# A convolution by FFT, a SiLU layer and a soft mixture of experts in one kernel: the exchange of the hidden layer's halves starts one chunk later, and one of its copies moves in every batch

## The chip, the cores and the metric

The kernel runs on one core of a Trainium2 chip. The metric is the device time of one execution in microseconds, the median of several runs.

## What is computed

The reference does three things in a row, all in 32-bit floats, on an input x of 8 batches, 3072 tokens and 256 channels:

```python
X = np.fft.rfft(x, axis=1)                    # convolution along the tokens, by a filter of frequencies
y = np.fft.irfft(X * (filt_r + 1j*filt_i)[None], n=3072, axis=1)
h = y.reshape(24576, 256) @ w_in              # hidden layer of 2048
z = (h / (1 + np.exp(-h))) @ w_out            # SiLU, back to 256
logits = z @ phi                              # 32 slots: 8 experts of 4
d = softmax(logits, axis=0)                   # over all 24576 tokens
s = (d.T @ z).reshape(8, 4, 256)              # what each slot sees
o = relu(s @ w1) @ w2                         # each expert on its 4 slots
out = softmax(logits, axis=1) @ o             # over the slots, for each token
```

## The kernel before

**Chunks.** The tokens are taken in 48 chunks of 512, six to a batch. For a chunk `c`, `mat4` (tile `py`) ends the inverse transform, and then come 16 blocks m = 0 to 15 of the hidden layer: `hidden` (six matmuls into `ph`, weights and activations split in a rounded part and a rest), `act` (ScalarE, SiLU, tile `g`) and `turn` (VectorE, transposes 32x32 blocks of `g` into the tile `X` of the chunk). `logits` (tile `pl`) sums `g` into 32 logits a token; they are exponentiated against a running maximum (tile `e`), go to DRAM (`ed`, function `spread0`) and come back spread over the partitions as `E` (`spread1`). `dsum` (tile `pd`) multiplies `E` with `X`, so that the sum over all tokens is taken of the hidden layer, and `update` adds it to `acc`. `dsum` of a chunk runs late in the next chunk, at its step 10.9.

**The exchange.** Where `swapped(c)` holds, the halves of `X` are exchanged between neighbouring groups of 32 partitions before `dsum`, so that it takes 32 products of 64x32 tiles of TensorE, eight at a time; elsewhere it takes 64 products of 32x32 tiles, 16 at a time. (A product of 32-bit floats counts as two instructions.) The exchange is made in two halves of eight blocks, and each half takes two copies of four blocks on GpSimd into the buffer `swap` (`swap_copy`, line 695), then two transfers `X<-X` (`swap_up`, line 699) and two transfers `X<-swap` (`swap_down`, line 704), issued by SyncE. There is one such buffer (tag S, 8 KB a partition): the third copy of a chunk waits until the `X<-swap` of its first half has been read. Before chunk 2 the same buffer holds `E_01`, the E of the chunks without exchange; the E of the others has a tag of its own and half the bytes.

**The convolution.** While the six chunks of a batch go through, the transform of the next batch is computed beside them (`fft_plan`). Its stage 2 runs in four groups Q = 0 to 3 of four tiles U: `mat2` (TensorE, tile `px`, from `a`, which comes from DRAM), `act2` (ScalarE, tile `sw`), `direct2` (VectorE, `y` from `px` and the filter `f`), `cross2` (GpSimd, `sw` times `f`, line 221) and `add2` (VectorE, `y` plus `sw`, line 360). Stage 3, `mat3` (tile `pb`), multiplies the four `y`. For Q = 0 stage 2 stands late in a batch's second chunk (c % 6 == 1) and its stage 3 early in the third.

**The order of the work.** It is written out by hand: `at(t, fn, ...)` notes a call with a time in steps, one step being one hidden block and 16 a chunk; the calls are sorted by t and issued in that order, and each engine works through its own instructions in order, as does the DMA queue of SyncE. So t is not a time but a place in each queue. In the second chunk of a batch, whose first step is `t0`, the copies stand at t0 + 7.7, 8.47, 12.5 and 16.47, the transfers up at t0 + 9.25 and 17.95, down at t0 + 11.2 and 19.35; the four cross products of Q = 0 stand at t0 + 12.5 (placed just ahead of the copy with the same time), 13.1, 14.0 and 14.2, their sums at 14.3, the stage 3 at 17.9.

The names of tiles in the profile are those given above; line 66 is the helper of all matmuls.

Of the kernel before, what the change touches and what calls it, by code (L numbers as in the profile page):

```python
# [9 lines left out]
F32 = mybir.dt.float32  # L10
# [7 lines left out]
P = 128  # L18
# [4 lines left out]
S = 32  # L23
# [4 lines left out]
CPB = NJ // JC  # L28
# [8 lines left out]
BUFS = dict(X=2, yT=2, g=11, L=2, nm=4, S=1, E2=2, lall=2, ct=1, cm=1,  # L37
            ld=3, c=2, ch=2, xh=2, a=1, f=2, y=2, ev8=1, bl=1, bp=1, dl=1, wt=3)
# [8 lines left out]
def fftconv_moe_softmoe(ctx, tc, x, cmat, chl, dmat, dmat0, emat, gmat, filt, sign, w_in, w_outT, w_out,  # L47
# [4 lines left out]
    NCHUNK = NB * CPB  # L52

    cst = ctx.enter_context(tc.tile_pool(name="cst", bufs=1))
    wk = ctx.enter_context(tc.tile_pool(name="wk", bufs=2))
# [9 lines left out]
    def mm(o, l, r, start, stop):  # L65
        T.matmul(o, lhsT=l, rhs=r, start=start, stop=stop)  # L66
# [75 lines left out]
    def at(t, fn, *args):  # L142
        plan.append((t, len(plan), fn, args))
# [542 lines left out]
    swap = {}  # L686

    def swapped(c):
        return 2 <= c < NCHUNK - 1

    def swap_copy(c, m):
        if m % 8 == 0:
# [65 lines left out]
    def spread1(c):  # L758
        if c == NCHUNK - 1:
            tail["S"] = wk.tile([P, 2048], F32, tag="S", bufs=BUFS["S"], name="tail_S")  # L760
            soft[c] = E = tail["S"][:, 0:512].rearrange("p (q f) -> p q f", q=4)
            t = et.pop(c)
            for q in range(4):
                pe = ps_h.tile([P, P], F32, tag="ph", name=f"pe_{q}")
                mm(pe, fold[S * q:S * q + S, :], t[S * q:S * q + S, 1], True, True)
                if q % 2:
                    V.tensor_copy(E[:, q, :], pe)
                else:
                    A.activation(E[:, q, :], pe, AF.Copy)
        elif not swapped(c):  # L770
            if c == 0:
                tail["E"] = wk.tile([P, 2, 4, P], F32, tag="S", bufs=BUFS["S"], name="E_01")
            soft[c] = E = tail["E"][:, c]
            ed = edt.pop(c)
            for a in range(4):
                DQ.dma_start(E[S * a:S * a + S], ed.rearrange("q i f -> i q f"))
        else:
            soft[c] = E = wk.tile([P, 2, P], F32, tag="E2", bufs=BUFS["E2"], name=f"E_{c}")
            ed = edt.pop(c)
            for a in range(4):  # L780
                h = 2 * (a % 2)
                DQ.dma_start(E[S * a:S * a + S], ed[h:h + 2].rearrange("q i f -> i q f"))
# [3 lines left out]
    def dsum(c):  # L786
        pdt[c] = {a: pool.tile([P, NM, 32], F32, tag=tag, name=f"pd_{c}_{a}")
                  for a, (pool, tag) in zip((0, 2, 1, 3), FOUR[:3] + ((ps_h, "ph"),))}
        X, E = xt.pop(c), soft[c]
        if not swapped(c):  # L790
            for B in range(4):
                for a in range(4):
                    s = slice(S * a, S * a + S)
                    for q in range(4):
                        mm(pdt[c][a][S * q:S * q + S], E[s, q, S * B:S * B + S], X[s, q // 2, :, 4 * (q % 2) + B, :],
                           B == 0, B == 3)
            return
        for x in range(2):
            for k in range(2):
                for R in range(2):  # L800
                    s = slice(64 * R, 64 * R + 64)
                    for g in range(4):
                        q, B = g % 2, g // 2 + 2 * k
                        mm(pdt[c][2 * R + x][S * g:S * g + S], E[s, q, S * B:S * B + S], X[s, x, :, 4 * q + B, :],
                           k == 0, k == 1)
# [67 lines left out]
    tail = {"w1": [], "w2": [], "t": []}  # L873
# [61 lines left out]
    for c in range(NCHUNK):  # L935
        t0 = 16 * c
        if c > 0:
            at(t0 - 16 + 6.9 if c < 3 or c % CPB == 0 else t0 - 19, loadd, c)
            at(t0 - 16 + 5.6 if c < 3 or c % CPB == 0 else t0 - 18.9, load3, c)
            at(t0 - 16 + 9.6 if c > 1 else 11.6, fly, c)  # L940
        ty = t0 - 16 + (VIS3 + 0.003 + (1.5 if c == 2 else 0) if c > 1 else 11.94) if c else -2
        for h in range(2):
            at(ty + 0.001 * h, mat4, c, h)
            at(ty + (0.002 * h + 0.01 if c else 0.2 * h + 0.55), out4, c, h)
        for m in range(NM):
            t = t0 + m
            late = c == 0 and m > 11
            at((11.8 + 0.01 * (m - 12) if m < 15 else 11.965) if late else t, hidden, c, m)
            at(11.97 + 0.001 * (m - 12) if c == 0 and m > 10 else t + (0.8995 if m in (1, 10) else 1.45 if (c, m) == (1, 11) else 1), act, c, m)
            te = max(t + 1.45 if m not in (1, 10) else t + 0.8996, (16.6 + 0.8 * (m - 5) if m > 4 else 11.7, 20.6 + 0.1 * m)[c] if c < 2 else 0)  # L950
            at(te, turn, c, m)
        copies, ups, downs = (((43.5, 43.6, 48.4, 48.47), (44.5, 49.95), (46.6, 51.35)) if c == 2 else
                              ((t0 + 7.7, t0 + 8.47, t0 + 12.5, t0 + 16.47), (t0 + 9.25, t0 + 17.95),
                               (t0 + 11.2, t0 + 19.35)))
        for i in range(4 if swapped(c) else 0):
            at(copies[i], swap_copy, c, 4 * i)
            if i < 2:
                at(ups[i], swap_up, c, 8 * i)
                at(downs[i], swap_down, c, 8 * i)
        at(t0 + VIS3 + 0.002 + (1.5 if c == 1 else 0) if c else 11.96, logits, c, 0)  # L960
        t1 = t0 + 16 + (VIS1 if c else 4.6)
        at(t1 + 0.002, logits, c, 1)
        if c == NCHUNK - 1:
            at(t1 + 0.0025, keep, 9)
        at(t1 + 0.003, soft0, c)
        if c < NCHUNK - 1:
            at(t1 + 0.00305, exp_early)
        at(t1 + 0.0031, soft1, c)
        at(t1 + 0.06, soft2, c)
        at(t1 + 1.1, soft3, c)  # L970
        if c < NCHUNK - 1:
            at(t1 + 1.5, spread0, c)
        at(t1 + (1.6 if swapped(c) else 3.3 if c < NCHUNK - 1 else 1.5), spread1, c)
        t3 = t0 + 16 + VIS3 + (1.5 if c == 0 else 0)
        at(t3, dsum, c)
        if c < NCHUNK - 1:
            at(t3 + 0.001, update, c)
        if c % 4 == 3:
            last = c == NCHUNK - 1
            if last:  # L980
                at(t0 + 16.95, exp_table)
            else:
                at(t1 + (11.2 if (c + 1) % CPB else 19.1), cprep, c // 4)
                at(t1 + {1: 43.8, 3: 27.8, 5: 19.1}[(c + 2) % CPB], cfin, c // 4)
                if c // 4 < NK - 2:
                    at(t1 + {1: 43.8, 3: 27.8, 5: 19.1}[(c + 2) % CPB] + 5, cstore, c // 4)
    E = mybir.EngineType
# [289 lines left out]
def _build(arrays):  # L1277
    import concourse.bacc as bacc

    nc = bacc.Bacc("TRN2", target_bir_lowering=False, num_devices=1, dynamic_dma_scratch_size=1024)  # L1280
    args = {}
    for name, a in arrays.items():
        args[name] = nc.dram_tensor(f"in_{name}_dram", a.shape, mybir.dt.from_np(a.dtype), kind="ExternalInput").ap()
    o = nc.dram_tensor("out_0_dram", arrays["x"].shape, F32, kind="ExternalOutput").ap()
    with tile.TileContext(nc, schedule_with_timeline_sim=True) as tc:  # L1285
        fftconv_moe_softmoe(tc, out=o, **args)
    return nc
# [10 lines left out]
```

## Time and profile before

| | us |
|---|---|
| median of 3 runs (1876.95 to 1885.63) | 1878.9 |
| the profiled execution | 1874.56 |
| its span, first to last instruction | 1872.4 |
| TensorE busy in it | 1799.6 (96%) |
| VectorE / ScalarE / GpSimd busy | 1278.1 / 953.7 / 450.2 |
| mean granted clock of TensorE | 0.979 |

In the profile PE is TensorE, DVE VectorE, ACT ScalarE, POOL GpSimd, SP SyncE, and SPq the instructions by which SyncE's queue issues transfers. A line gives the place in the kernel, the engine, the operation and the tiles as "written<-read". "Idle before" is the time in which the engine stood still ahead of an instruction, and behind the arrow stands what ended it. The granted clock is a share of full speed.

### The profile page before, as it was taken

How to read it: one execution, taken by the hardware profiler on the slowest of the kernel's cores; microseconds unless marked ns; L12 is line 12 of the kernel's file. 1: busy time of each engine (PE TensorE's matmuls, PEld its weight loads, DVE VectorE, ACT ScalarE, POOL GpSimd, SP SyncE). 2: the span in 40 equal slices, each digit the busy share in tenths (PEclk: the TensorE clock that was granted, in tenths of full speed). 3: DMA queues.
4: the chain of work that ended last, by engine and by line, in shares of the span. 5: the costliest groups of instructions: out<-in, count | busy, mean ns of one | idle time of the engine just before them, and what ended most of it. 6: DMA issues, size and time to landing. Idle time of an engine off the chain costs nothing. (4 is left out here: it accounts for less than half of the span.)

```text
span 1872.4 us, 45508 instructions
## 1 busy us (share of the span) xinstructions
PE 1799.6 (96%) x18538; PEld 1347.2 (72%) x18538; DVE 1278.1 (68%) x2279; ACT 953.7 (51%) x1831; POOL 450.2 (24%) x380
## 2 busy tenths in 40 slices
PE   7899999999999999989999999999999999999995
PEld 6677577767776778767786777767786777777754
DVE  3597677678667766677676876677667776776543
ACT  2554556456455556456455556456554645454433
POOL 0201323133132323232232323232332321111000
PEclk9899999999999999999999999999999999999996
DMA  9965657676677658776486647676586655445689
GB/s 323 316 214 172 190 152 234 196 213 179 174 214 206 184 142 229 213 210 188 138 246 198 200 123 226 211 204 204 140 240 180 201 157 157 120 142 144 228 313 397
DMA packets 210932, 379.91 MB, mean 203 GB/s; under 512 B 24508, under 2 KB 130724, under 8 KB 196004
## 3 DMA queue, kind: packets, MB, share of 16 engines
q1 hardware_dynamic: 177244, 330.46, 58.5%
q10 hardware_dynamic: 33480, 46.56, 7.5%
q8 instruction: 146, 2.39, 0.5%
q14 instruction: 62, 0.51, 0.1%
HBM read 192.82 MB, written 91.83 MB: 152 GB/s over the span
## 5 line engine op out<-in xcount | busy, mean ns | idle before, releaser
L66 PE MATMUL ph<-yT,w_hl 128*128 128x512 f32 x4608 | 1092.4, 393 | 0.6 <-DVE yT L653 0.2
L66 PEld LDWEIGHTS ph<-yT,w_hl 128*128 128x128 f32 x4608 | 852.4, 188 | 200.9 <-issue 27.3
L684 DVE STREAM_TRANSPOSE X<-g 128x512 f32<-128x512 f32 x768 | 517.0, 696 | 233.7 <-ACT g L674 229.7
L674 ACT ACTIVATE g<-ph 128x512 f32<-128x512 f32 x768 | 450.1, 602 | 337.5 <-PE ph L66 256.0
L695 POOL COPY swap<-X 128x1024 f32<-128x1024 f32 x180 | 198.0, 1101 | 773.7 <-DVE X L684 514.7
L221 POOL TENSOR_TENSOR sw<-sw,f 128x512 f32<-128x512 f32 x123 | 162.1, 1332 | 401.6 <-ACT sw L215 385.1
L66 PEld LDWEIGHTS pl<-g,wp 128*32 128x32 f32 x6144 | 164.2, 111 | 71.8 <-issue 66.3
L652 ACT ACTIVATE yT<-py 128x512 fp32r<-128x512 f32 x96 | 57.3, 597 | 308.7 <-PE py L66 308.7
L66 PE MATMUL pl<-g,wp 128*32 128x128 f32 x6144 | 190.6, 276 | 0.6 <-DVE wp L138 0.6
L66 PE MATMUL pd<-X,E 64*32 64x512 f32 (+1 forms) x3136 | 178.5, 597 | 4.6 <-DMA E<-ed 4.4
L812 DVE SCALAR_TENSOR_TENSOR acc<-acc,nm,pd 128x512 f32<-128x512 f32 x184 | 124.9, 734 | 9.2 <-PE pd L66 9.1
L66 PEld LDWEIGHTS pd<-X,E 64*32 64x32 f32 (+1 forms) x3136 | 57.8, 107 | 99.4 <-issue 89.8
L360 DVE TENSOR_TENSOR y<-y,sw 128x512 f32<-128x512 f32 x112 | 106.7, 992 | 21.1 <-POOL sw L221 21.1
L279 POOL TENSOR_TENSOR xh<-x,xh 128x512 fp32r<-128x512 f32 x72 | 92.9, 1290 | 116.0 <-DVE xh L278 97.5
L653 DVE TENSOR_TENSOR yT<-py,yT 128x512 fp32r<-128x512 f32 x96 | 66.3, 691 | 71.9 <-ACT yT L652 71.9
L218 DVE TENSOR_TENSOR y<-px,f 128x512 f32<-128x512 f32 x124 | 82.0, 679 | 33.9 <-PE px L66 28.4
L370 ACT ACTIVATE eb<-pb 128x512 f32<-128x512 f32 x112 | 57.8, 603 | 41.2 <-PE pb L66 41.2
L214 ACT ACTIVATE sw<-px,sg 128x256 f32<-128x256 f32 x123 | 60.0, 488 | 32.7 <-PE px L66 14.5
L66 PE MATMUL py<-d,b 128*128 128x128 f32 x416 | 65.8, 282 | 5.5 <-DMA b<-hop 4.7
L66 PEld LDWEIGHTS pa<-xh,ch 128*128 128x128 f32 x432 | 61.1, 189 | 10.7 <-POOL xh L279 4.4
L66 PE MATMUL pa<-xh,ch 128*128 128x256 f32 x432 | 64.8, 283 | 2.6 <-POOL xh L279 2.4
L66 PE MATMUL pb<-y,gm 32*32 32x512 f32 (+1 forms) x1008 | 50.9, 654 | 14.1 <-DVE y L360 14.1
(157 smaller groups left out, 1346.5 us busy)
## 6 DMA issues: line engine op xcount, KB each, us to landing
X<-X SPq DMA_DIRECT2D x180, 256.0 KB, 3.7
X<-swap SPq DMA_DIRECT2D x180, 256.0 KB, 4.2
f<-in_filt_dram SPq DMA_DIRECT2D x128, 256.0 KB, 4.1
a<-s SPq DMA_DIRECT2D x64, 512.0 KB, 5.4
s<-eb SPq DMA_DIRECT2D x60, 512.0 KB, 5.1
out_dram<-ots SPq DMA_DIRECT2D x23, 1024.0 KB, 11.9
b<-s SPq DMA_DIRECT2D x160, 128.0 KB, 4.9
x<-in_x_dram ACTq DMA_DIRECT2D x72, 256.0 KB, 5.0
```

The lines of the kernel that those rows point to most:

```text
L66: T.matmul(o, lhsT=l, rhs=r, start=start, stop=stop)
L214: A.activation(sw[:, 0, :], p[:, 1, :], AF.Copy, scale=sg[:, s:s + 1])
L218: V.tensor_tensor(y, p, f[:, 0, :].unsqueeze(1).to_broadcast([P, 2, CH]), op=ALU.mult)
L221: G.tensor_tensor(sw, sw, f[:, 1, :].unsqueeze(1).to_broadcast([P, 2, CH]), op=ALU.mult)
L279: G.tensor_tensor(h[:, 1, :], tf, h[:, 0, :], op=ALU.subtract)
L360: V.tensor_tensor(y, y, st.pop(("sw", Q, U)), op=ALU.add)
L370: A.activation(st["eb"][:, q], p, AF.Copy)
L653: V.tensor_tensor(y[:, half, 1, :], py, y[:, half, 0, :], op=ALU.subtract)
L674: A.activation(g, pht.pop((c, m)), AF.Silu)
L684: V.transpose(xt[c][:, :, m].rearrange("p h b j -> p h (b j)"), gt[c, m].rearrange("p (h f) -> p h f", h=2))
L695: G.tensor_copy(t[:, m % 8:m % 8 + 4], xt[c][:, 0, m:m + 4].rearrange("p m b j -> p m (b j)"))
L812: V.scalar_tensor_tensor(out=acc[:, :, a, :], in0=acc[:, :, a, :], scalar=mrun[c][:, 3:4], in1=p, op0=ALU.mult, op1=ALU.add)
```

## The change

Three edits in the written order, no new function. The exchange starts with chunk 3 instead of 2. Chunk 2's E goes into the tile of the chunks 0 and 1, which gets a third part, and its `dsum` takes 16 tiles; by the rule for such chunks its `spread1` stands 1.7 steps later. Chunk 3's exchange, now the first, gets the special times that chunk 2's had: its first two copies stand behind chunk 2's `dsum` (step 58.9). And in every second chunk of a batch from chunk 7 on the third copy moves from t0 + 12.5 to t0 + 16.465, next to the fourth.

```diff
     def swapped(c):
-        return 2 <= c < NCHUNK - 1
+        return 3 <= c < NCHUNK - 1
...
         elif not swapped(c):
             if c == 0:
-                tail["E"] = wk.tile([P, 2, 4, P], F32, tag="S", bufs=BUFS["S"], name="E_01")
+                tail["E"] = wk.tile([P, 3, 4, P], F32, tag="S", bufs=BUFS["S"], name="E_012")
             soft[c] = E = tail["E"][:, c]
...
-        copies, ups, downs = (((43.5, 43.6, 48.4, 48.47), (44.5, 49.95), (46.6, 51.35)) if c == 2 else
-                              ((t0 + 7.7, t0 + 8.47, t0 + 12.5, t0 + 16.47), (t0 + 9.25, t0 + 17.95),
-                               (t0 + 11.2, t0 + 19.35)))
+        copies, ups, downs = (((59.5, 59.6, 63.5, 64.47), (60.4, 65.95), (62.2, 67.35)) if c == 3 else
+                              ((t0 + 7.7, t0 + 8.47, t0 + (16.465 if c % CPB == 1 else 12.5), t0 + 16.47),
+                               (t0 + 9.25, t0 + 17.95), (t0 + 11.2, t0 + 19.35)))
```

## Rows read from the trace of the kernel before

**Rows 1.** TensorE's waits: engine, tile, releaser, us in total, times, longest
```profile
PE pb L66 <- DVE y L360: 14.1, 12, 2.2
```
**Rows 2.** Timeline, PE, 371 to 403: start, us, instructions, idle before
```profile
371.09 8.48 PE L66 MATMUL ph<-yT,w_hl 128*128 128x512 f32 x36
380.72 1.09 PE L66 MATMUL pb<-y,gm 32*32 32x256 f32 x16 [1.15 <-DVE y L360]
382.99 1.94 PE L66 MATMUL pb<-y,gm 32*32 32x512 f32 x18 [1.18 <-DVE y L360]
...
387.52 1.17 PE L66 MATMUL px<-a,em 24*32 24x512 f32 x32
...
401.08 2.38 PE L66 MATMUL pd<-X,E 64*32 64x512 f32 x40
```
**Rows 3.** Timeline, DVE, same stretch
```profile
375.32 0.65 DVE L360 TENSOR_TENSOR y<-y,sw 128x512 f32<-128x512 f32 x1
378.91 4.02 DVE L360 TENSOR_TENSOR y<-y,sw 128x512 f32<-128x512 f32 x3 [2.94 <-POOL sw L221]
382.86 3.07 DVE L684 STREAM_TRANSPOSE X<-g 128x512 f32<-128x512 f32 x5
```
**Rows 4.** Timeline, POOL, same stretch
```profile
372.19 1.29 POOL L221 TENSOR_TENSOR sw<-sw,f 128x512 f32<-128x512 f32 x1 [12.63 <-ACT sw L215]
376.59 1.04 POOL L695 COPY swap<-X 128x1024 f32<-128x1024 f32 x1 [3.11 <-DMA X<-swap]
377.59 4.19 POOL L221 TENSOR_TENSOR sw<-sw,f 128x512 f32<-128x512 f32 x3
384.81 1.04 POOL L695 COPY swap<-X 128x1024 f32<-128x1024 f32 x1 [3.02 <-DVE X L684]
```
**Rows 5.** Timeline, ACT, same stretch: the last input of a cross product
```profile
374.74 0.53 ACT L215 ACTIVATE sw<-px,sg 128x256 f32<-128x256 f32 x1
```
**Rows 6.** Timeline, SP's queue, same stretch
```profile
372.28 1.58 SPq L704 DMA_DIRECT2D X<-swap  x2
...
379.81 0.93 SPq L194 DMA_DIRECT2D a<-s  x2
...
397.60 1.74 SPq L782 DMA_DIRECT2D E<-ed  x4
```
**Rows 7.** Six stages: stretch and us, PE busy, clock, DMA share, GB/s
```profile
...
797.12:828.14 31.02, 26.10 (x230) 1.00 0.66 194
...
1435.74:1466.08 30.34, 27.71 (x229) 0.94 0.69 206
sum 181.16, PE 162.76; mean PE 27.13
```
**Rows 8.** Timeline, PE, the next chunk, 411 to 435
```profile
418.09 1.14 PE L66 MATMUL pb<-y,gm 32*32 32x512 f32 x32
...
434.60 0.66 PE L66 MATMUL pd<-X,E 64*32 64x512 f32 x8
```
**Rows 9.** Timeline, PE, 140 to 228: `pd` of chunks 1 and 2
```profile
177.07 4.46 PE L66 MATMUL pd<-X,E 32*32 32x512 f32 x128
220.81 6.45 PE L66 MATMUL pd<-X,E 64*32 64x512 f32 x64 [3.03 <-DMA E<-ed]
```
**Rows 10.** Timeline, POOL and SP's queue, the last of the six places
```profile
1449.76 1.04 POOL L695 COPY swap<-X 128x1024 f32<-128x1024 f32 x1 [3.02 <-DVE X L684]
...
1461.05 1.75 SPq L782 DMA_DIRECT2D E<-ed  x4
```
**Rows 11.** Timeline, DVE and SP's queue, chunk 2's e, ed and E
```profile
204.24 0.31 DVE L745 STREAM_TRANSPOSE e<-e 128x128 f32<-128x128 f32 x1 [0.61 <-ACT e L737]
...
215.28 0.53 SPq L756 DMA_DIRECT2D ed<-e  x1
218.30 1.98 SPq L782 DMA_DIRECT2D E<-ed  x4
```
**Rows 12.** Timeline, POOL, 181 to 184: chunk 2's first copies
```profile
181.66 2.02 POOL L695 COPY swap<-X 128x1024 f32<-128x1024 f32 x2 [8.49 <-PE pd L66]
```

## The prediction

> **What bounds the kernel now.** I read the page first: TensorE is busy for 96% of the span, so time is won only where TensorE stands still or runs at a lower granted clock. The table of what TensorE waited for comes next. Its largest entry is `pb`, the products of stage 3, which waits for VectorE's sums `y`: 14.1 us in 12 waits [rows 1]. In order of time these are two waits in each of six places, always in the chunk after a batch's second one (chunks 8, 14, 20, 26, 32 and 38). So I laid out the first place engine by engine.
>
> TensorE: a block of 36 hidden products from 371.09 to 379.57, then 1.15 us of waiting, half of `pb`, 1.18 us of waiting, the other half; `px` at 387.52, `pd` at 401.08 [rows 2]. VectorE: one sum `y` at 375.32 in 0.65 us, then 2.94 us idle on GpSimd, then three sums in 4.02 us, then five overdue transposes until 385.93 [rows 3]. GpSimd gives the reason: one cross product at 372.19, then 3.11 us idle in front of an exchange copy that waits for the landing of a transfer `X<-swap`, then the copy, and only at 377.59 the three other cross products [rows 4]. ScalarE had written the last of their inputs by 375.27 [rows 5]. SyncE issued that transfer at 372.28 [rows 6]. The copy needs the one buffer `swap` back; the products queued behind it don't.
>
> What this costs is read from whole stages. From the start of such a block of 36 to `pd` the six stages take 181.16 us, 30.19 on average [rows 7]. The chunk after has the same work in the same order without a wait: `pb` to `pd` 16.51 us [rows 8], and with the 8.48 of the block 24.99. So 6 x (30.19 - 24.99) = 31.2 us is lost in all. Besides the waits for `y` that holds waits of `px` for its input `a`, and the clock: four of the six stages ran at a mean of 0.94, two at 1.00 (one of either kind stands in [rows 7]). A mean of 0.94 over 30 us is some 3.5 us at the lower level (1.2 instead of 2.4 GHz), 1.8 us lost.
>
> The second place is chunk 2's `pd`: 3.03 us of waiting for E, then 6.45 us of products, together 9.48 [rows 9].
>
> **The change part by part.** *Third copy moved, chunks 7 to 37.* It goes behind the three cross products and stands beside the fourth copy. (It moves in chunk 43 too, where no cross product is behind it and nothing is to be won.) Nothing is added. Times from here count from the start of the 36 products (371.09 = 0).
> The first cross product ends at 2.4; its successors follow at once instead of at 6.5, and the last input, there at 4.2, is in time for the fourth at 5.0. The row of three sums shows sums and products side by side: from 377.59 to 382.93, 5.34 us for three of each, where a sum alone took 0.65 [rows 3, 4]. So three of each are through at 2.4 + 5.3 = 7.7; the fourth sum adds 0.65, and the moved copy, which now falls between the sums, 0 to 1.04: 8.4 to 9.4. TensorE is ready for `pb` at 8.5 and needs the last sums half a microsecond later. The waits of 1.15 and 1.18 shrink to 0 to 0.4.
> The Trainium skill (SBUF — State Buffer, "Who interferes with whom") speaks against the place chosen: a VectorE instruction with two SBUF inputs and a GpSimd one that reads SBUF shut each other out for a whole instruction. By that the copy costs its full 1.04, the upper of the two ends; 4.02 for three sums against 0.65 for one bears it out.
> Next in line is `px`. SyncE issued `a` at 379.81, 0.93 after the second cross product ended, because the load of `f` before it waits for that product's buffer [rows 6]; `px` came 7.7 us later. The second product now ends at 3.7, `a` is issued at 4.6, `px` comes at 12.3 and `pd` 13.56 later [rows 2], at 25.9: 0.9 above the floor.
> Then E. VectorE's transposes of blocks 13 to 15 follow the sums: 9.4 + 1.9 = 11.3 (in the trace 13.7), and there the fourth copy starts. The moved copy has run by then, so it delays nothing in the exchange. From the fourth copy's start to the end of E's last issue the first place took 14.5 us, the last 13.0 [rows 4, 6, 10]. Landing adds 0.5 to 1.7: chunk 2's `pd`, which waited for E, began 0.5 after the issue [rows 9, 11], chunk 7's, which did not wait, 1.7 after. So E is there at 24.8 to 27.5, and `pd` moves from 30.2 to about 26.3, with 25.0 as the floor and 27.5 as the late end. What bounds it then is E, with `a` right beside it. Gain 6 x 3.9 = 23 us (16 to 31).
>
> *Chunk 2 without exchange.* Removed: four copies of 1.04 us on GpSimd, which has room, and eight transfers of 256 KB. In SyncE's queue `ed` was issued at 215.28, behind the exchange's transfers, though VectorE had e transposed at 204.55 [rows 11]. Without them it goes at about 205; from its issue to the last of E took 5.0 us, so E is there around 211, also with twice the bytes and 1.7 steps later in the plan (chunk 1's E is of that kind, and its `pd` did not wait [rows 9]). TensorE wants it at 217.78. The wait goes. The sum in 16 tiles has no row for chunk 2; chunk 1's took 4.46 for its 128 instructions, and I bound it by that and by today's 6.45. I take 4.46, the same form: 9.48 - 4.46 = 5.0 (3.0 at the other end).
> Here the Trainium skill (TensorE: Matmul & The Clock Gate, "Step-by-step: what each phase is for") gives a dearer price: about 62 ns of sequencer time for each matmul when hardware decoding is off. By it 128 would take 7.9 us and this part would save 1.5; the row's 35 ns each speaks against it.
>
> *E_012 and chunk 3's copies.* The tile grows within a buffer whose size the swap tiles set already. Chunk 3's first copy must now wait until chunk 2's `pd` has read E, as chunk 2's copies wait today behind chunk 1's (8.49 us idle on GpSimd [rows 12]). Behind it on GpSimd stands the last cross product of Q = 2. `pd` ends at 217.78 + 4.46 = 222.2, the copy at 223.3, the product at 224.6; its stage 3 stands over six steps later in the plan, so nobody waits. Behind the `X<-X` of these copies on SyncE stand loads of f, d and b for the next chunks but one, with as much room. The second half can be copied only when the first half's transfers have come back, so copies three and four follow each other instead of the transposes: at most 2 x 1.04 us on the way to chunk 3's E. I give back 0.5 (0 to 2).
>
> **Sum.** 23 + 5.0 - 0.5 = 27.5 us. The profiled execution took 1874.56 (span 1872.4 and 2.2 around it), so 1847.1. The median of the runs is 1878.9, 4.3 above it; what is saved is saved there too: 1851.
>
> **The rivals.**
> *At the floor.* Nothing is late next: E's chain shortens because the loads of f, d, a and b leave 4 us earlier and are gone when `X<-X` goes out. 31.2 + 5.0 = 36.2, so 1843. Against it: E's last issue ended 1.7 us before `pd` already in the first place. 0.18.
> *Chunk 2 doesn't do it.* E late for another reason, or the sum at 6.45 and chunk 3 late by 2: that part gives 0 to 1, so 1855. 0.08.
> *E takes the wait over.* E at 29 instead of 26.2, and some of the waits with a lower clock behind them: 6 x 1.2 + 4 = 11, so 1868. 0.07.
> *No effect.* The cross products are late for another reason than the copy. Against it: all three ran back to back once the copy was through. 1879. 0.03.
> *Slower.* The exchange lengthens: its transfers `X<-X` and `X<-swap` of the second half, sent nearer to the loads of `a` and `b`, take 5 us more each way. E then comes at 36, each of the six stages takes 6 us more than today, and 36 - 4.5 = 31 us are lost: 1910. It decides from the point where E is later than 30.2 + 0.8. Against it: `a` and `b` leave 4 us earlier, `X<-X` only 2. 0.03.
> The forecast itself has 0.61.
>
> **How the numbers follow.** Low end: the floor, 1842. High end: E at 27.5 in all six (16 us), a fall of the clock left in two (-3.6), chunk 2's sum at 6.45 with 1.5 given back (1.5): 14 us, so 1865. From 1842 to 1865 holds the forecast, the floor and the second rival with their edges lost, about 0.8. Half a per cent, 9.4 us, is about what a measurement here tells from none. Faster by more: 0.61 + 0.18 + 0.08 and a part of the E rival, 0.90; within it 0.07; slower 0.03.
>
> **What would show it.** In the changed kernel's trace: three cross products right behind the first in chunks 7, 13 and so on; no wait of `pb` for `y` over 0.5 us; a clock of 1.00 in most of the six stages and their sum near 158; chunk 2's `pd` as 128 instructions in 4.5 us without a wait. It would be wrong if `pd` in those six stages waits for E by over 2 us, if sums still wait for GpSimd by microseconds, or if chunk 3's `pd` is late.

## The result, and the profile after

The change takes 1848.4 us, the median of 4 runs (1845.09 to 1850.08), against 1880.1 of the kernel before (4 runs, 1876.95 to 1885.63): a ratio of 0.983 (95% interval 0.981 to 0.985), 31.7 us less. The forecast was 1851, with 1842 to 1865 as its range. The profiled execution took 1849.11 (span 1847.0, mean granted clock 0.984); that of before, 1874.56, lay 5.5 below the median of its runs, so the two traces differ by 25.4 only.

TensorE's table of waits comes first (engine, tile, releaser: us in total, times, longest). `pb` behind `y`, the largest entry of before [rows 1], is gone; `px` behind its input `a` is now the first (8 waits; before 4 with 10.2 us). In the six places alone it waits 7.6 us in five of them, before 4.3 in three:

```profile
PE px L66 <- DMA a<-s: 14.7, 8, 5.3
...
PE pd L66 <- DMA E<-ed: 0.4, 1, 0.4
```

The first of the six places, TensorE (start, us, instructions, idle before), answers to [rows 2]. `pb` follows the block of 36 at once; `px` waits 2.14 us; `pd` comes without a wait:

```profile
369.02 8.45 PE L66 MATMUL ph<-yT,w_hl 128*128 128x512 f32 x36
377.40 1.98 PE L66 MATMUL pb<-y,gm 32*32 32x256 f32 x34
379.30 1.95 PE L66 MATMUL pl<-g,wp 128*32 128x128 f32 x64
383.39 1.33 PE L66 MATMUL px<-a,em 24*32 24x512 f32 x32 [2.14 <-DMA a<-s]
384.65 13.91 PE L66 MATMUL ph<-yT,w_hl 128*128 128x512 f32 x54
398.50 1.95 PE L66 MATMUL pd<-X,E 64*32 64x512 f32 x32
```

GpSimd and VectorE there (against [rows 3, 4]), GpSimd first: four cross products in a row, the moved copy behind them, the sums through at 378.23, 9.2 us after the block's start:

```profile
370.12 5.52 POOL L221 TENSOR_TENSOR sw<-sw,f 128x512 f32<-128x512 f32 x4 [12.63 <-ACT sw L215]
375.89 1.19 POOL L695 COPY swap<-X 128x1024 f32<-128x1024 f32 x1 [0.26 <-DMA X<-swap]
380.10 1.04 POOL L695 COPY swap<-X 128x1024 f32<-128x1024 f32 x1 [3.02 <-DVE X L684]
```

VectorE's sums and the transposes behind them, same stretch:

```profile
373.26 4.97 DVE L360 TENSOR_TENSOR y<-y,sw 128x512 f32<-128x512 f32 x4
378.15 3.07 DVE L684 STREAM_TRANSPOSE X<-g 128x512 f32<-128x512 f32 x5
```

SyncE's queue there (against [rows 6]) shows why `px` waits: ahead of `a` stand the exchange's transfers, two loads of `f` and one of `d`, each for its issue time.

```profile
371.30 1.14 SPq L704 DMA_DIRECT2D X<-swap  x2
372.61 1.51 SPq L332 DMA_DIRECT2D f<-in_filt_dram  x2
374.22 0.44 SPq L605 DMA_DIRECT2D d<-in_dmat_dram  x1
374.75 0.93 SPq L194 DMA_DIRECT2D a<-s  x2
...
393.62 1.74 SPq L782 DMA_DIRECT2D E<-ed  x4
```

The six stages (stretch and us, PE busy, clock, DMA share, GB/s; [rows 7] had a sum of 181.16). Only the first is still at a lower clock:

```profile
369.02:398.50 29.48, 27.34 (x230) 0.94 0.73 218
579.45:607.53 28.08, 25.79 (x230) 1.00 0.72 216
790.85:818.52 27.67, 25.76 (x230) 1.00 0.72 215
1000.21:1026.75 26.54, 25.79 (x229) 1.00 0.75 220
1207.70:1234.00 26.30, 25.77 (x229) 1.00 0.75 225
1415.15:1440.90 25.75, 25.75 (x230) 1.00 0.77 227
sum 163.82, PE 156.21; mean PE 26.04
```

Chunk 2's `pd` as 128 instructions without a wait (against [rows 9]), and chunk 3's behind it, which waits 0.42 us and then takes 4.71 (64 such instructions took 3.66 elsewhere, as in the trace of the earlier `a` below):

```profile
219.10 4.47 PE L66 MATMUL pd<-X,E 32*32 32x512 f32 x128
...
254.03 4.71 PE L66 MATMUL pd<-X,E 64*32 64x512 f32 x64 [0.42 <-DMA E<-ed]
```

GpSimd between them (against [rows 12]): chunk 3's first copies stand behind that `pd`, the other two behind the landing of `X<-swap`:

```profile
223.69 1.04 POOL L695 COPY swap<-X 128x1024 f32<-128x1024 f32 x1 [4.13 <-PE pd L66]
224.69 1.28 POOL L221 TENSOR_TENSOR sw<-sw,f 128x512 f32<-128x512 f32 x1
225.91 1.04 POOL L695 COPY swap<-X 128x1024 f32<-128x1024 f32 x1
239.68 2.02 POOL L695 COPY swap<-X 128x1024 f32<-128x1024 f32 x2 [12.73 <-DMA X<-swap]
```

### The profile page after: what moved, and what is told of

It is laid out like the page before. It is cut to its first block, busy times and chain, and to the rows that moved or that the text cites. A ratio compares the mean times of both kernels' runs of the same rounds, so it can differ in the third digit from the quotient of the medians.

```text
span 1847.0 us, 45612 instructions
## 1 busy us (share of the span) xinstructions
PE 1789.1 (97%) x18602; PEld 1344.1 (73%) x18602; DVE 1278.1 (69%) x2279; ACT 955.2 (52%) x1831; POOL 447.3 (24%) x376
## 3 DMA queue, kind: packets, MB, share of 16 engines
q1 hardware_dynamic: 177116, 328.49, 58.9%
## 5 line engine op out<-in xcount | busy, mean ns | idle before, releaser
L812 DVE SCALAR_TENSOR_TENSOR acc<-acc,nm,pd 128x512 f32<-128x512 f32 x184 | 125.0, 734 | 10.4 <-PE pd L66 10.2
L214 ACT ACTIVATE sw<-px,sg 128x256 f32<-128x256 f32 x123 | 59.9, 487 | 33.7 <-PE px L66 14.4
L66 PEld LDWEIGHTS py<-d,b 128*128 128x128 f32 x416 | 56.0, 196 | 7.9 <-issue 6.9
## 6 DMA issues: line engine op xcount, KB each, us to landing
out_dram<-ots SPq DMA_DIRECT2D x23, 1024.0 KB, 12.3
```

Of the source, the lines that this page charges most:

```text
L214: A.activation(sw[:, 0, :], p[:, 1, :], AF.Copy, scale=sg[:, s:s + 1])
L812: V.scalar_tensor_tensor(out=acc[:, :, a, :], in0=acc[:, :, a, :], scalar=mrun[c][:, 3:4], in1=p, op0=ALU.mult, op1=ALU.add)
```

## The experiments

A chunk's length is counted below from the start of its hidden products to that of the next chunk's. The table sums these lengths, in us, for each trace; in the kernels named "repeat" nothing is changed against the one named ahead of it.

| trace | 3, 4 | 8, 14, ... 38 | 7, 13, ... 37 | 17, 23 | 29, 35 | span |
|---|---|---|---|---|---|---|
| before | 74.95 | 232.91 | 205.06 | 67.85 | 69.57 | 1872.4 |
| before, repeats | 74.71, 76.31 | 237.98, 238.81 | 205.18, 205.55 | 67.87, 68.85 | 72.08, 72.53 | 1878.7, 1881.7 |
| third copy alone | 75.78 | 223.01 | 206.90 | 68.77 | 70.33 | 1865.8 |
| its repeat | 75.23 | 214.71 | 206.22 | 69.09 | 70.56 | 1855.2 |
| chunk 2 alone | 71.53 | 229.94 | 202.37 | 69.52 | 67.81 | 1860.4 |
| its repeat | 71.85 | 234.15 | 201.98 | 69.57 | 67.81 | 1864.8 |
| after | 71.55 | 215.53 | 202.60 | 69.41 | 67.83 | 1847.0 |
| `a` earlier | 71.26 | 204.93 | 203.61 | 69.53 | 67.81 | 1836.1 |
| and chunk 3's copies | 70.99 | 204.17 | 202.13 | 69.23 | 67.85 | 1831.9 |

**The third copy alone.** The kernel before with this one edit, so the change without its part on chunk 2:

```diff
-                              ((t0 + 7.7, t0 + 8.47, t0 + 12.5, t0 + 16.47), (t0 + 9.25, t0 + 17.95),
+                              ((t0 + 7.7, t0 + 8.47, t0 + (16.465 if c % CPB == 1 else 12.5), t0 + 16.47), (t0 + 9.25, t0 + 17.95),
```

> Only the third copy of chunks 7 to 43 is moved behind the cross products; chunk 2 keeps its exchange. My theory: the two parts are independent, and the six stages carry most of the gain. In the changed kernel's trace they take 163.8 us against 181.2, so I expect 17 us less in the trace and a time 17 to 27 us below the kernel before (ratio 0.986 to 0.991), no wait of the stage-3 products for their sums, and chunk 2's pd still waiting 2 to 4 us for E. The rival, that chunk 2 is the larger part or that the copies only help together with it, expects less than 10 us.

Measured: 1860.3 (ratio 0.990, 0.987 to 0.993), 18.6 less than before. No `pb` waits for `y`; `px` waits for `a` in all six places (0.42 to 4.14 us), `pd` for E in none of them. The six stages took 169.5 us, and 160.8 in the repeat, against 181.2, 186.1 and 186.7 in the three traces of before. Chunk 2's `pd` still waited 3.5 us for E. So this part works as it was described, and what follows it is `a`.

**Chunk 2 alone.** The change (the line taken out below) with the third copy where it was:

```diff
-                              ((t0 + 7.7, t0 + 8.47, t0 + (16.465 if c % CPB == 1 else 12.5), t0 + 16.47),
+                              ((t0 + 7.7, t0 + 8.47, t0 + 12.5, t0 + 16.47),
```

> Only chunk 2 loses its exchange (and chunk 3's copies move); the third copy of the second chunks stays where it was. My theory: pd of chunk 2 takes 9.5 us with its wait before and 4.5 after, chunk 3's pd gives back 1.5, so 3 to 4 us less, ratio 0.997 to 0.999, and the stages with the late cross products unchanged at 29 to 31 us each. The rival that the parts need each other expects either nothing or over 8 us here.

Measured: 1862.7 (0.992, 0.990 to 0.993), 16.1 less: four times what was expected. In chunks 3 and 4 the traces show what was expected, 3.6 us (75.3 to 71.7, means of the table's rows); the rest comes elsewhere. The time lies where the rival stood that the parts need each other (over 8 us), but alone they save 18.6 and 16.1, together 34.7, against 31.7 of the whole change, and 3 us are within the intervals; so they don't. This miss is taken up below.

**`a` earlier.** To see whether `a` is what bounds the six stages after the change, and not E, its load for Q = 1 goes ahead of the exchange's transfers in SyncE's queue:

```diff
-            at(tx[Q - 1] + 2 if Q else t1[-1] + (2.2 if b == 1 else 4), load2, Q)
+            at((t0 + 27.15 if b > 1 and Q == 1 else tx[Q - 1] + 2) if Q else t1[-1] + (2.2 if b == 1 else 4), load2, Q)
```

> The changed kernel, and the load of a for Q = 1 of batches 2 to 7 stands at t0 + 27.15 (behind the products that free its buffer, ahead of the transfer down of the exchange) instead of two steps later behind three loads of f. My theory: what is left in the six stages is a, held in SyncE's queue by the exchange and by loads of f; a is issued at 0.2 to 1 us from the stage's start instead of 4.6 to 6.1, the waits of px (0.5 to 2.3 us) go, and the stages end when E is there, at 24.9 to 27.5: their sum falls from 163.8 to 151 to 158, the time by 5 to 12 us against the changed kernel. The rival, that E is the true bound right behind a, expects waits of pd for E as long as the px waits that go, and less than 3 us. A second rival, that the transfers themselves are slow whatever their order, expects px still to wait by over 1 us.

Measured: 1838.2 (0.979, 0.977 to 0.980), another 10 us less. SyncE's queue and TensorE in the first place, whose block of 36 starts at 368.08: `a` leaves 0.25 us behind that, `px` comes at 11.39 and `pd` at 24.93, both without a wait.

```profile
368.33 1.52 SPq L194 DMA_DIRECT2D a<-s  x2
369.95 1.16 SPq L704 DMA_DIRECT2D X<-swap  x2
...
389.16 1.74 SPq L782 DMA_DIRECT2D E<-ed  x4
```

TensorE in that kernel, same place:

```profile
379.47 1.14 PE L66 MATMUL px<-a,em 24*32 24x512 f32 x32
380.54 12.54 PE L66 MATMUL ph<-yT,w_hl 128*128 128x512 f32 x54
393.01 3.66 PE L66 MATMUL pd<-X,E 64*32 64x512 f32 x64
```

All six stages stand at a granted clock of 1.00, and their sum is near the prediction's floor of 6 x 24.99 = 150. The last line of their table:

```profile
sum 151.15, PE 150.20; mean PE 25.03
```

E, issued by 390.90, is there. In three of the six `pd` waits for it by 0.07 to 0.52 us: so E does come next, but at the floor and not above it. The rival "at the floor" needed this step too.

**Chunk 3's copies sooner.** On top of it, chunk 3's first two copies together and their transfers half a step earlier:

```diff
-        copies, ups, downs = (((59.5, 59.6, 63.5, 64.47), (60.4, 65.95), (62.2, 67.35)) if c == 3 else
+        copies, ups, downs = (((59.5, 59.51, 63.5, 64.47), (59.8, 65.95), (62.2, 67.35)) if c == 3 else
```

> As the kernel with the early load of a, and chunk 3's first two copies stand next to each other ahead of the last cross product of Q = 2, with their transfers up at 59.8, ahead of a load of f. My theory: chunk 3's pd lost 1.5 us because its first exchange started late; copies and transfers are 1.3 to 2.5 us earlier, pd takes 3.7 instead of 4.7 and does not wait, so 0.5 to 1.5 us less than that kernel, which only the trace can resolve. The rival, that the second half waits for transfers that are slow anyway, expects pd of chunk 3 unchanged.

Measured: 1836.3 (0.978, 0.976 to 0.979), the fastest of the versions, though 1.9 below the one ahead of it is within both intervals. Chunk 4 takes 34.64 instead of 34.91 (35.17 after the change), where 0.5 to 1.5 were expected: chunk 3's `pd` didn't fall to 3.7 us without a wait but took 4.53 behind a wait of 0.17 (4.38 behind 0.58 in the version ahead), so the 1.9 are not shown to come from this edit.

**Repeats.** Before, chunk 2 alone and the third copy alone once more, to tell what a single trace is worth:

> The kernel before once more, unchanged, for a second trace. Its runs lie at 1879 us in the median and its traced execution at 1874.6, while the kernel with the chunk-2 part alone gained 16 us where the traces of chunks 3 and 4 give 3.4. If the rest is a matter of which execution was traced, this trace is some 4 us longer than the first one, in the six stages (181.2 us there) or in the clock, and not in chunks 3 and 4. If the rest is real and local, chunk 3 takes well over 41.4 us here.

> A third trace of the kernel before, for the spread between executions of one program: by the theory of chance the chunks that differ between these three are those after second chunks and single waits, by 1 to 3 us each, and chunks 3 and 4 agree within 1 us.

> The kernel with the chunk-2 part alone once more: by the theory of chance its six stages lie in the same spread as those of the kernel before (175 to 188 us in all three traces of it), chunk 3 at 36.4 and chunk 4 at 35.2. If the part does something lasting, the stages or the low-clock time are shorter here in both traces than in all of the kernel before.

> The kernel with the moved copy alone once more: six stages between 160 and 172 us, with the waits of px for a as what varies, and chunk 3 at 41 to 43 us as in the kernel before.

Measured: 1880.9, 1883.9, 1866.9 and 1857.4. The six chunks with the waits (8 to 38) scatter by 4 to 8 us between executions of one program. Two other columns part by whether chunk 2 has an exchange: chunks 7 to 37 (205.1 to 206.9 with it, 202.0 to 203.6 without) and 29 and 35 (69.6 to 72.5, 67.8). Chunks 17 and 23 lean the other way by less than they scatter (67.9 to 69.1, 69.2 to 69.6). So dropping chunk 2's exchange changes chunks that come up to 35 chunks later.

One thing that differs there is the wait of ScalarE's own queue for its loads of `x` and `c`. Chunk 35 on ScalarE, in the second repeat of before and with chunk 2 alone: the load of `c` leaves 15.6 us after the chunk's start (1341.14) in the one and 13.6 after it (1327.01) in the other, and `g` stands behind it.

```profile
1354.45 0.41 ACTq L254 DMA_DIRECT2D x<-in_x_dram  x1
1356.76 0.34 ACTq L258 DMA_DIRECT2D c<-in_chl_dram  x1
1357.14 1.09 ACT L674 ACTIVATE g<-ph 128x512 f32<-128x512 f32 x2 [3.85 <-DMA x<-in_x_dram]
```

The same three instructions with chunk 2 alone:

```profile
1339.37 0.39 ACTq L254 DMA_DIRECT2D x<-in_x_dram  x1
1340.62 0.36 ACTq L258 DMA_DIRECT2D c<-in_chl_dram  x1
1341.02 1.09 ACT L674 ACTIVATE g<-ph 128x512 f32<-128x512 f32 x2 [1.86 <-DMA ed<-e]
```

With chunk 2 alone, what ended ScalarE's wait is the landing of `ed`, a transfer of SyncE's queue that neither `c` nor `g` reads. The built programs say why: the transfers of both queues take eight completion counts in turn, in the program's order, and an issue may carry a wait for the transfer eight places ahead of it. With chunk 2 alone the load of `c` in chunk 35 stands eight places behind `ed`; in the kernel before it stands eight places behind E, which goes out 3.5 us later. (For that wait the profile names `x`; the program has the load of `c` wait for the first transfer of E.) Of 1491 transfers that both programs have, 95 stand eight places behind another one than before, 58 of them around these loads in chunks 5 to 35. The eight transfers that chunk 2 lost are no reason by themselves, being a whole turn of the eight counts. Each queue's own order is the same from chunk 5 on; what changed is how the program interleaves the two queues, and what decides that stays open. With the third copy alone this order is that of the kernel before.

That wait is not what TensorE mostly feels. In chunk 35 its wait is `py` for VectorE's `acc`: 2.04 us in the second repeat of before, none with chunk 2 alone. VectorE's `acc` stands behind its first sum with `b` (line 635, tile `bp`), and that sum waits until SyncE's loads of `b` have landed. It starts 21.46 to 23.28 us after the chunk's start in the three traces of before, and at 19.74 and 19.93 with chunk 2 alone, though `b` begins to leave at 15.2 to 15.9 in all five. The lengths of chunks 5, 11, 17, 23, 29 and 35 in all fourteen traces, 84 in number, follow this start: where it comes by 20.5 us a chunk takes 33.91, and where it comes later, it is longer by as much. In 71 of the 84 this holds within 0.03 us. Ten are 0.1 to 1.0 longer than that; the largest excess is in chunk 17 without chunk 2's exchange, where `c` stands behind E and TensorE's `ph` waits for `g` by 0.72 to 1.05. The three over 37 us are 1.6 longer than that, and the granted clock fell in them. Why `b` lands later isn't shown.

**The places of these loads.** The load of `x` and `c` for hidden block 1 is one number of the written order (`tl`, the second: t0 - 9.6). 0.8 earlier in before, no such load stands behind an E; 1.4 later, one stands behind E in each of chunks 5, 11, 17, 23, 29 and 35.

```diff
-            tl = [t0 + d for d in (-14.3, -9.6, -4.7, -3.6, -1.9, -1.2, 0.5, 1.5, 6.5, 7.5, 11.3, 12.4)]
+            tl = [t0 + d for d in (-14.3, -10.4, -4.7, -3.6, -1.9, -1.2, 0.5, 1.5, 6.5, 7.5, 11.3, 12.4)]
```

> The kernel before, with one plan entry changed: the loads of x and c for hidden block 1 of a batch go 0.8 us earlier (-10.4 instead of -9.6). Why: in the program every transfer, over SyncE's and ScalarE's queues together, takes one of eight completion counts in turn, so its issue stands until the transfer eight places earlier in the program's order has landed. In the kernel before the load of c for chunks 29 and 35 falls eight places behind that chunk's E and stands in ScalarE's queue until E has landed; those two chunks take 34.98 and 36.42 us (means of three traces) where the kernels without chunk 2's exchange take 33.91. Here no such load is behind an E any more (it is behind an X<-swap or an earlier one). Theory of the shared counts: chunks 29 and 35 at 33.9 each, chunk 17 at 33.9 to 34.3, together 3.6 us less, and something on top in the chunks that follow them: 1872 to 1877 against 1879. Rival, chance from execution to execution, or chunk 2 alone: chunks 29 and 35 stay at 34.7 to 37, the time within 2 us of before.

Measured: 1884.2 (1.003, 1.001 to 1.005); a miss. Chunks 29 and 35 fell, to 34.33 and 34.28, but 5, 11, 17 and 23 rose to between 34.67 and 35.19 with no load of block 1 behind an E. The first sum with `b` started at 20.89 to 21.75 in all six; in chunk 11 it did so at 21.25, where `c` had left at 10.72 and `g` didn't wait for it.

```diff
+            tl = [t0 + d for d in (-14.3, -8.2, -4.7, -3.6, -1.9, -1.2, 0.5, 1.5, 6.5, 7.5, 11.3, 12.4)]
```

> The kernel before, the same plan entry 1.4 us later (-8.2): now the loads of x or c for hidden block 1 stand eight places behind that chunk's E in all of chunks 5, 11, 17, 23, 29 and 35, in the last two also the load of x. Theory of the shared counts: chunks 5, 11, 17 and 23, which take 33.9 to 34.3 in the kernel before, rise to 34.3 to 36 as well, 29 and 35 stay at 34.7 to 37 or more, 3 to 8 us more in all: 1882 to 1890. Rival: no such pattern, 1877 to 1881.

Measured: 1884.5 (1.002, 1.000 to 1.005), in the expected range (but so did the shift the other way) and in the expected places: 34.11 (chunk 5), 34.49, 35.07, 35.17, 37.92 and 38.13 (35). Chunk 35 started at 1342.18. SyncE's queue, where E leaves at 1356.52 and `b` 16.17 after the start:

```profile
1356.52 1.74 SPq L782 DMA_DIRECT2D E<-ed  x4
1358.35 2.42 SPq L623 DMA_DIRECT2D b<-s  x4
```

ScalarE in the same chunk, with the load of `c` at 1359.10 and `g` behind it (the profile names `ph` for the wait, but the load's issue ends at 1359.44, 0.05 ahead of `g`):

```profile
1359.10 0.34 ACTq L258 DMA_DIRECT2D c<-in_chl_dram  x1
1359.49 0.60 ACT L674 ACTIVATE g<-ph 128x512 f32<-128x512 f32 x1 [3.79 <-PE ph L66]
```

TensorE in the same chunk, where `py` comes 2.54 us late:

```profile
1368.53 0.49 PE L66 MATMUL py<-d,b 128*128 128x128 f32 x2 [2.54 <-DVE acc L812]
```

VectorE there, whose first sum with `b` starts 23.11 after the chunk's start:

```profile
1365.29 0.48 DVE L635 SCALAR_TENSOR_TENSOR bp<-b,sg 128x256 f32<-128x256 f32 x1 [3.45 <-DMA b<-s]
1367.77 2.68 DVE L812 SCALAR_TENSOR_TENSOR acc<-acc,nm,pd 128x512 f32<-128x512 f32 x4
```

The same in chunk 35 with chunk 2 alone (started at 1327.01), where `b` left 15.44 after the start, the sum comes at 19.74, and no `py` waits:

```profile
1342.45 2.42 SPq L623 DMA_DIRECT2D b<-s  x4
...
1346.75 0.48 DVE L635 SCALAR_TENSOR_TENSOR bp<-b,sg 128x256 f32<-128x256 f32 x1 [2.76 <-DMA b<-s]
1349.23 2.68 DVE L812 SCALAR_TENSOR_TENSOR acc<-acc,nm,pd 128x512 f32<-128x512 f32 x4
```

So `b` left 0.73 later and was used 3.37 later.

The same shift (-8.2) with chunk 2 alone:

> Chunk 2 without exchange alone (the third copy where it was), and the same plan entry 1.4 us later (-8.2). All chunks 5, 11, 17, 23, 29 and 35 have a load of c behind that chunk's E; without the shift only 17 and 23 have (35.1 and 34.5 us), and 29 and 35 take 33.91. Theory of the shared counts: what chunk 2's part gave behind chunk 4 came in with the places of those loads, so chunks 29 and 35 rise to 34.7 to 37, 5 and 11 above 33.9 too, and 3 to 8 us of its 16 are gone: 1866 to 1871 against 1863. Rival, the gain has another cause: chunks 29 and 35 at 33.91, 1861 to 1865.

Measured: 1867.8 (0.995, 0.994 to 0.997), 5 us more than without the shift, as expected, though the single repeat without it took 1866.9 too. Chunks 29 and 35 stayed at 33.93 and 34.21, against the expectation, and 5, 11, 17 and 23 took 34.31, 34.46, 35.01 and 35.16. In 29 and 35 the load of `c` did stand behind E, and `g` waited 2.76 and 3.46 us; the first sum with `b` came at 20.42 and 20.78, and so little was lost.

The earlier place (-10.4) in the fastest version:

> The fastest so far (the change, a batch's second load of a issued earlier, chunk 3's copies sooner; 1836.3), and the loads for hidden block 1 0.8 us earlier (-10.4), so that none of them is behind an E. There chunks 17 and 23 took 34.95 and 34.28 and the others 33.9. Theory of the shared counts: chunks 17 and 23 at 33.9 too, 1.3 us less: 1833 to 1836. Rival: no change in these chunks, 1835 to 1838.

Measured: 1837.9 (0.980, 0.977 to 0.982), no difference in the time, which is the rival's. Chunks 17 and 23 take 33.93 each instead of 34.95 and 34.28, as expected; chunk 11 rose by 0.7 and chunks 7 to 37 by 0.9 together. Chunks 17, 23 and 29 in it (columns as for the six stages):

```profile
681.66:715.59 33.93, 33.93 (x349) 1.00 0.77 227
888.72:922.64 33.92, 33.92 (x349) 1.00 0.75 219
1095.51:1129.44 33.93, 33.93 (x349) 1.00 0.78 231
```

What follows: moving these loads in the order of all transfers moves time between chunks, by up to some 4 us in one (38.13 against 33.91), of which 1.6 came with a lower clock. That is shown, and so is the wait that ends last in most of these chunks, the landing of `b`. That the wait of ScalarE's queue is the cause is not: a load behind E cost nothing in chunk 29 of the last but one version, and other chunks lost 0.8 without one.

Chunk 2's unexpected 12 us are placed only in part. Between the means of before and of chunk 2 alone, chunks 29 and 35 give 3.6 (`b` lands sooner) and chunks 7 to 37 give 3.1, while 17 and 23 take 1.4 back; with 3.6 in chunks 3 and 4 that is 8.9 of 16. In chunks 7 to 37 what differs is a wait of `pa` for GpSimd's `xh`, which is made of the loads of `x`: single waits of 0.95 and 0.96 us in the first trace of before and four of 0.66 to 0.96 in the third, none over 0.32 in the two traces with chunk 2 alone, but one of 0.96 again after the change; what delays `xh` wasn't traced. Of the rest, 4.5 lie in chunks 8 to 38, whose length scatters by more than that, and stay open.

## Why the prediction held, step by step

**The waits for `y`.** As predicted: the three products follow the first at once, the last sum ends at 9.2 in all six places (8.4 to 9.4 foreseen), and no `pb` waits. After the change the copy ran among the sums (1.19 us in the first place), so the upper end applied. In the version with `a` earlier it fell behind the sums in the first place, and they were through 8.35 after the start, the lower end:

```profile
372.31 4.12 DVE L360 TENSOR_TENSOR y<-y,sw 128x512 f32<-128x512 f32 x4
```

So the copy cost 0.86. That is the side on which the Trainium skill (SBUF — State Buffer, "Who interferes with whom") stood, by which a copy on GpSimd and a sum on VectorE shut each other out. The trace agrees: a sum alone took 0.68 us, and the one beside the copy 1.52, from 376.11 to 377.63, ending 0.55 behind the copy (377.08); the sums beside the last two products, too, ended 0.55 behind them.

**`a` and `px`.** This is the term that was mis-sized. The step said: the second product ends at 3.7, `a` leaves at 4.6, `px` comes 7.7 later at 12.3. The product did end at 3.7. But `a` left at 5.7 to 6.1 in three places, behind two loads of `f` and one of `d`, and at 4.6 to 4.7 in the others, and `px` came 8.2 to 8.6 us behind it in the five where it waited: at 14.4, 14.5, 14.1, 13.0, 12.8 and, without a wait, 12.2; the waits were 2.29 to 0.53. The prediction took the distance from product to `a` from a place where the exchange's transfers and the first load of `f` had already gone. There the issue of the second `f` took 0.33 us; in these three places it stood right behind the first and took 0.97 to 1.00.

**E.** "What bounds it then is E, with `a` right beside it" was the wrong way round. E never made `pd` wait in the six stages, and with `a` earlier they went to 151.2.

**The six stages.** 163.8 us instead of 158: 17.3 less than the trace of before, where the step had 23 (16 to 31). Against the mean of three traces of before, 184.7, it is 20.8. The places of `px`, each with the 13.56 from `px` to `pd`, make 162.3 of it; the clock came back as foreseen but for one stage at 0.94, which makes the other 1.5.

**Chunk 2.** `ed` left at 205.91 (foreseen 205; [rows 11] had 215.28), the last of E at 211.03 (211), `pd` took 4.47 without a wait: chunk 3 went from 41.44 to 36.38, 5.06 for a term of 5.0. The row's 35 ns for each instruction held, and not the 62 of the Trainium skill (TensorE: Matmul & The Clock Gate, "Step-by-step: what each phase is for"), which that page gives for hardware decoding off.

**Chunk 3's copies.** The term was 0.5 given back (0 to 2); chunk 4 went from 33.51 to 35.17, 1.66. The bound "at most 2 x 1.04" for copies three and four was wrong: they started at 239.68, 4 us behind the last transpose (ended 235.73), because the first half's `X<-swap` left only at 233.28, behind loads of `f`, `d` and `b`, and landed 5.2 later. So what was said to have "as much room" took room from the exchange, and the sign "chunk 3's `pd` is late" did show, in a small way.

**The sum.** 17.3 + 5.06 - 1.66 = 20.7, where 27.5 stood. The traces differ by 25.4; the other 4.7 are chunks 6 to 36 and 7 to 37 (5.6 together), 29 and 35 (1.7), less what 17, 23 and the rest took back (2.6). Against the medians the change gave 31.7, since the profiled execution of before was a short one. So the mechanism of the largest term held, but the nearness of 1851 to 1848.4 is in part luck: the terms were 6.8 too large together, and an effect that the forecast didn't know and a short trace of before made up for it.

## What to carry to other kernels

When a queue's head is freed, walk the queue again from there: the next thing late is whatever stands between the freed instruction and the consumer, with each issue counted, and here that was 1.1 to 1.5 us of loads in front of `a`. Before a remainder is explained, run the same program a few more times: the stages with waits moved by 6 us between executions, as much as the miss in the largest term. And where transfers of two queues share completion counts, an edit in one place can change what an issue waits for many chunks later, so compare that in both programs. But a wait that is found so is not yet a cost: follow TensorE's own wait back to what ended last, which here was mostly the landing of `b` and not the load that stood in ScalarE's queue.

## What was not expected of the hardware

A load on ScalarE's queue can stand until a transfer of SyncE's queue that it has nothing to do with has landed, and ScalarE's arithmetic behind it stands too: 1.86 us behind `ed` with chunk 2 alone, 3.85 behind E in a repeat of before. The issue of one load of `f` took 0.33 us of SyncE's queue in the first place before, 1.00 there after the change and 1.70 with `a` ahead of it: the issue times in front of a late load are not constants. The sums of `y` took 0.65 us alone [rows 3] and 4.97 for four beside GpSimd's products and copy.
